# Attention over pooled keys with a gated MLP: first two batches in another order, identity matmuls as steps of their own

## The chip, the core and the metric

The kernel runs on one core of a Trainium2 chip. The core has TensorE (PE, matmuls; its weight loads are listed apart as PEld), VectorE (DVE), ScalarE (ACT), GpSimd (POOL) and SyncE (SP, which here only issues transfers), each with a queue of its own that is worked off in order, and semaphores between them. The metric is the device time of one execution in microseconds, the median of several; lower is better.

## The reference

Inputs are q, k and v (8 batches, 8 heads, 576 tokens, 64 wide) and two weight matrices (512 x 2048 and 2048 x 512), all float32. Keys and values are averaged over groups of 8 tokens, so each head has 72 keys; then attention, then an MLP on the 4608 tokens.

```
k_p = k.reshape(B, H, Sp, pool, D).mean(axis=3)
v_p = v.reshape(B, H, Sp, pool, D).mean(axis=3)
scores = scale * np.matmul(q, k_p.transpose(0, 1, 3, 2))
...
attn = attn / (np.sum(attn, axis=-1, keepdims=True) + 1e-09)
return np.matmul(attn, v_p).astype(np.float32)
...
h = x @ w_in
g = h * (1.0 / (1.0 + np.exp(-1.702 * h)))
return (g @ w_out).astype(np.float32)
```

## The kernel before

**Tiling.** A batch's 512 first tokens are one chunk of the MLP; the 64 left over of each batch make a ninth chunk. Chunks 0 and 1 run through `dense`: for each 128 hidden units f, twelve matmuls `h<-x,w` (three products for each of four quarters of the model width, since both operands are split into a high and a low float32r part), the gelu on ACT, and per 128 tokens three matmuls `o<-w,gh` and `o<-w,gl`. The other chunks take a form with fewer products on pairs of f (`ha`, `hb`, `o<-w,ghall`). Chunk 0 can't begin before batch 0's attention has ended, and the weights for it are decoded on ACT, DVE and POOL as they arrive (`raw`, `e`, `w`).

**Attention of batch 0**, in plain float32 (each matmul is two passes in the trace): `tps` sums the last 64 tokens' keys and values (L1556; DVE makes `tbd` of it); `red_k`, `red_v` sum groups of tokens by matmuls with the identity (L1420; DVE makes `kbd` and `vbd`); `qps` turns the queries (L1699), copied to `qt`; `kps` turns the keys (L1607, L1613), copied by ACT to `k`; `sps` are the scores (L1727); DVE and ACT make the softmax of a piece of the tokens from four `sps` (`nm`, `sc`, `main`, `tail`); `apt` and `tpt` turn the weights (L1871), and `pav` multiplies with the values (L1974, L1977), which become `x`. Names end in batch-free numbers: `sps_0_2` is piece 0, pair of heads 2. Piece 0 has 256 tokens, piece 1 has 320.

**What sets the order.** Every step is a task with an engine and a due time. `Plan.order` lays them out by a planner; then each task's rank is its place in that list plus a number from the table `PLACES`, a table `SWAPPED` moves a step to another engine (a copy from ACT to DVE, a subtraction from POOL to DVE), and the tasks are written out by rank. Each engine's queue follows that order.

**Matmuls of the identity.** `keep_warm` (L2600) multiplies the identity by itself into a bank of PSUM, `warm`, that chunk 0 uses later; nothing reads the product. One such matmul is a task, due first of all. Others are put in as the tasks are written out, ahead of the tasks that `WARMS` names: 16 ahead of `tps`, 2 ahead of the first `qps`, 2 ahead of the first `h`. That makes 21, in the trace 42 passes.

Of the kernel before, what the change touches and what calls it, by code (L numbers as in the profile page):

```python
# [1103 lines left out]
def attention_moe_kernel(ctx: ExitStack, tc: tile.TileContext, q, k, v, w_in, w_out, out):  # L1104
# [1562 lines left out]
    with tc.manual_schedule():  # L2667
        for t in order:
            for _ in range(WARMS.get(t.name, 0)):
                keep_warm()  # L2670
# [31 lines left out]
```

## Time and profile before

| | |
|---|---|
| time, median of 3 runs | 890.97 us (890.58 to 892.03) |
| the profiled execution's own time | 892.42 us |
| its span, first to last instruction | 890.6 us |
| PE busy | 879.3 us (99%) |
| DVE, ACT, POOL busy | 71%, 61%, 35% |

A matmul's record runs on while its result drains, so records of consecutive matmuls overlap: the spacing of their starts is what one costs when they follow each other, and the length of one record is more. A row of the timeline merges consecutive instructions of one kind: its start, the time to the end of the last one, and their count, with the idle time ahead of it in brackets.

### The profile page before, as it was taken

The page shows a single profiled execution, that of the slowest core. Times are in us where ns is not written, and L with a number is a line of the kernel's source. Part 1 is how long each engine was busy: PE and PEld are TensorE (multiplying, and loading weights), DVE is VectorE, ACT ScalarE, POOL GpSimd, SP SyncE. Part 2 cuts the span into 40 slices and gives each one's busy share as a digit, 9 for nine tenths or more (in the row PEclk, how much of TensorE's full clock was granted, in tenths as well). Part 3 has the DMA queues.
Part 4 walks back from the last instruction along what each step waited for, and adds up shares of the span by engine and source line. Part 5 has one row for each costly group of instructions (what it writes and reads, how often), then busy time and mean ns, then how long its engine had stood idle before and what let it go on. Part 6 is the DMA issues. An engine that isn't in the chain of part 4 may idle for free.

```text
span 890.6 us, 15774 instructions
## 1 busy us (share of the span) xinstructions
PE 879.3 (99%) x5432; PEld 785.8 (88%) x5432; DVE 630.1 (71%) x1255; ACT 543.8 (61%) x1245; POOL 314.6 (35%) x309
## 2 busy tenths in 40 slices
PE   7999999999999999999999999999999999999997
PEld 6889988888899998898999998989998989998986
DVE  5877889888888886698878887787677843222332
ACT  4986665356676754667576766686568563344433
POOL 2888565664412233221521161236323460000000
PEclk9999999999999999999999999999999999999999
DMA  9964454657467657678775677667664675556541
GB/s 254 370 223 134 124 151 156 234 200 215 156 202 228 223 181 245 182 226 241 219 218 181 176 233 219 220 203 250 175 205 145 201 235 186 172 190 205 166 142 48
DMA packets 145262, 176.67 MB, mean 198 GB/s; under 512 B 85664, under 2 KB 96928, under 8 KB 145184
## 3 DMA queue, kind: packets, MB, share of 16 engines
q1 hardware_dynamic: 140336, 166.89, 60.5%
q10 hardware_dynamic: 4848, 8.78, 2.8%
q8 instruction: 43, 0.70, 0.3%
q14 instruction: 35, 0.29, 0.1%
HBM read 150.47 MB, written 25.17 MB: 197 GB/s over the span
## 4 chain that ended last, share of the span: by engine, by line
PE 94%; SPq 2%; ACT 1%; DMA 1%; issue 0%; DVE 0%; ACTq 0%
PE ha L2435 18%; PE hb L2435 13%; PE o L2639 12%; PE o L2638 12%; PE o L2637 11%; PE sps L1727 4%; PE h L2230 3%; PE h L2232 3%; PE h L2231 3%; PE o L2274 3%; PE o L2272 3%; PE o L2273 3%; DMA raw<-in_moe_w_out_dram 1%; SPq L1317 1%; PE pav L1966 1%; PE pav L1969 1%
## 5 line engine op out<-in xcount | busy, mean ns | idle before, releaser
L2639 PE MATMUL o<-w,glall 128*128 128x512 f32 x448 | 176.3, 394 | 0.0
L2637 PE MATMUL o<-w,ghall 128*128 128x512 f32 x448 | 176.3, 394 | 0.0
L2638 PE MATMUL o<-w,ghall 128*128 128x512 f32 x448 | 176.0, 393 | 0.0
L2489 POOL TENSOR_TENSOR glall<-shared,ghall 128x256 fp32r<-128x256 f32 x88 | 70.4, 805 | 215.8 <-ACT shared L2482 144.3
L2639 PEld LDWEIGHTS o<-w,glall 128*128 128x128 f32 x448 | 84.2, 188 | 18.5
L2435 PEld LDWEIGHTS ha<-xs,ws 128*128 128x128 f32 x672 | 92.6, 189 | 7.6 <-ACT shared L2450 1.0
L2435 PE MATMUL ha<-xs,ws 128*128 128x256 f32 x672 | 99.2, 283 | 0.0
L2474 ACT ACTIVATE ghall<-shared 128x256 fp32r<-128x256 f32 x150 | 61.5, 415 | 60.9 <-DVE shared L2457 32.5
L2435 PE MATMUL hb<-x,ws 128*128 128x256 f32 x672 | 95.5, 284 | 0.0
L2435 PEld LDWEIGHTS hb<-x,ws 128*128 128x128 f32 x672 | 89.1, 189 | 4.5 <-DVE shared L2457 0.5
L2637 PEld LDWEIGHTS o<-w,ghall 128*128 128x128 f32 x448 | 84.6, 189 | 9.1
L2638 PEld LDWEIGHTS o<-w,ghall 128*128 128x128 f32 x448 | 84.1, 188 | 9.1
L2457 DVE TENSOR_TENSOR shared<-shared,hb 128x256 f32<-128x256 f32 x112 | 46.5, 415 | 55.8 <-PE hb L2435 40.9
L2450 ACT COPY shared<-ha 128x256 f32<-128x256 f32 x94 | 34.8, 370 | 65.0 <-PE ha L2435 63.8
L2489 POOL TENSOR_TENSOR glall<-gall,ghall 128x256 fp32r<-128x256 f32 x45 | 33.4, 746 | 103.4 <-ACT gall L2482 67.9
L2230 PE MATMUL h<-x,w 128*128 128x256 f32 (+1 forms) x192 | 63.0, 328 | 0.7 <-ACT g L2247 0.5
L2482 ACT ACTIVATE shared<-shared 128x256 f32<-128x256 f32 x150 | 61.0, 415 | 3.7 <-ACT osb L2190 0.5
L2232 PE MATMUL h<-x,w 128*128 128x256 f32 (+1 forms) x192 | 61.3, 319 | 0.0
L2231 PE MATMUL h<-x,w 128*128 128x256 f32 (+1 forms) x192 | 61.2, 319 | 0.0
L2260 POOL TENSOR_TENSOR gl<-g,gh 128x512 fp32r<-128x512 f32 x30 | 41.0, 1367 | 50.4 <-ACT gh L2252 35.6
L2489 DVE TENSOR_TENSOR glall<-shared,ghall 128x256 fp32r<-128x256 f32 x62 | 29.5, 477 | 35.8 <-ACT shared L2482 27.3
L2435 PEld LDWEIGHTS ha<-x,shared 128*128 128x128 f32 x336 | 46.7, 189 | 4.8 <-ACT shared L2450 0.8
(193 smaller groups left out, 2039.1 us busy)
## 6 DMA issues: line engine op xcount, KB each, us to landing
ws<-wd SPq DMA_DIRECT2D x168, 512.0 KB
shared<-wd SPq DMA_DIRECT2D x56, 256.0 KB
out_dram<-osb ACTq DMA_DIRECT2D x32, 256.0 KB
wd<-stage SPq DMA_DIRECT2D x16, 512.0 KB
raw<-in_moe_w_in_dram SPq DMA_DIRECT2D x15, 512.0 KB
raw<-in_moe_w_out_dram SPq DMA_DIRECT2D x15, 512.0 KB
kv_False<-in_k_dram SPq DMA_DIRECT2D x28, 256.0 KB
kv_True<-in_v_dram SPq DMA_DIRECT2D x28, 256.0 KB
```

Source lines behind the costliest of these rows:

```text
L2230: nc.tensor.matmul(o, lhsT=w[:, 0, j], rhs=xs[:, 0], start=j == 0, stop=False)
L2231: nc.tensor.matmul(o, lhsT=w[:, 1, j], rhs=xs[:, 0], start=False, stop=False)
L2232: nc.tensor.matmul(o, lhsT=w[:, 0, j], rhs=xs[:, 1], start=False, stop=j == NJ - 1)
L2260: engine.tensor_tensor(out=gl(), in0=g(), in1=gh().bitcast(F32), op=ALU.subtract)
L2435: nc.tensor.matmul(o, lhsT=wv()[:, r, jj], rhs=xo(k, jj), start=start and n == 0, stop=n == len(terms) - 1,  skip_group_check=not start,)
L2457: lambda: nc.vector.tensor_tensor(out=part(i), in0=part(i), in1=hb()[:, half * 256 : half * 256 + 256], op=ALU.add),
L2474: lambda: nc.scalar.activation(out=gh(), in_=src(), func=AF.Gelu_apprx_sigmoid),
L2482: lambda: nc.scalar.activation(out=part(i), in_=src(), func=AF.Gelu_apprx_sigmoid),
L2489: engine.tensor_tensor(out=gl(), in0=part(i), in1=gh().bitcast(F32), op=ALU.subtract)
L2637: nc.tensor.matmul(o(), lhsT=gh()[:, tok], rhs=w()[:, 0], start=start, stop=False)
L2638: nc.tensor.matmul(o(), lhsT=gh()[:, tok], rhs=w()[:, 1], start=False, stop=False)
L2639: nc.tensor.matmul(o(), lhsT=gl()[:, tok], rhs=w()[:, 0], start=False, stop=stop)
```

## The change

The table `WARMS` and its use are gone. `keep_warm` now writes four matmuls instead of one, and 28 such steps are planned, 112 matmuls, where before there were 21. Each step has a place in `PLACES` of its own: steps 0 to 12 have no entry, 13 to 27 have one. The rest of the table is another one for the steps of batches 0 and 1 and of chunk 0, and so is `SWAPPED`.

```diff
-WARMS = {"PE tps0#0": 16, "PE qps0_0#0": 2, "PE h0_0#0": 2}
...
+    "PE tpt0_0#0": -5.6667, "PE tpt1_0#0": 59.8444, "PE tpt1_1#0": 101.0, "PE warm#13": 42.3333,
+    "PE warm#14": 56.3333, "PE warm#15": 96.0, "PE warm#16": 93.2, "PE warm#17": 89.8, "PE warm#18": 101.5,
...
     def keep_warm():
-        nc.tensor.matmul(warm()[:, 0:P], lhsT=ident, rhs=ident, start=True, stop=True)
-
-    pe(WARM, keep_warm, [], [warm], due=-100.0)
+        for _ in range(4):
+            nc.tensor.matmul(warm()[:, 0:P], lhsT=ident, rhs=ident, start=True, stop=True)
+
+    for _ in range(28):
+        pe(4 * WARM, keep_warm, [], [warm], due=-100.0)
...
         for t in order:
-            for _ in range(WARMS.get(t.name, 0)):
-                keep_warm()
             t.emit()
```

On PE the program begins, before, with 17 identity matmuls, and batch 0's keys follow:

```order
L2600 MATMUL warm<-ident 128x128 x17
L1556 MATMUL tps_188<-tl_148,members 128x512
L2600 MATMUL warm<-ident 128x128 x2
L1699 MATMUL qps_0_0_196<-ident,q_0_151 128x128 x2
L1699 MATMUL qps_0_1_199<-ident,q_0_151 128x128 x2
L1607 MATMUL kps_0_202<-ident,kbd_190 128x64x2 x2
L1613 MATMUL kps_0_202<-ident,tbd_192 128x4x8 x2
L1727 MATMUL sps_0_0_215<-k_211,qt_0_0_207 128x144 x2
```

The same place on PE after the change (32 or 33 is added to the lines):

```order
L2633 MATMUL warm<-ident 128x128 x56
L1588 MATMUL tps_220<-tl_195,members 128x512
L2633 MATMUL warm<-ident 128x128 x4
L1731 MATMUL qps_0_0_227<-ident,q_0_214 128x128 x2
L1731 MATMUL qps_0_1_230<-ident,q_0_214 128x128 x2
L1639 MATMUL kps_0_237<-ident,kbd_206 128x64x2 x2
L1645 MATMUL kps_0_237<-ident,tbd_235 128x4x8 x2
L1452 MATMUL red_k_247<-kv_208,ident 128x128 x8
L1759 MATMUL sps_0_0_257<-k_244,qt_0_0_242 128x144 x2
```

Ahead of `tps` now stand 56 identity matmuls instead of 17, and the second half of the keys' sums (`red_k`) has moved up, ahead of the first scores.

On PE between the last scores of batch 0's piece 0 and the turning of its softmax (`apt`), before:

```order
L1727 MATMUL sps_0_2_274<-k_211,qt_0_2_241 128x144 x2
L1727 MATMUL sps_0_3_279<-k_211,qt_0_3_270 128x144 x2
L1420 MATMUL red_v_287<-kv_165,ident 128x128 x8
L1699 MATMUL qps_1_0_309<-ident,q_1_168 128x128 x2
L1699 MATMUL qps_1_0_309<-ident,q_2_170 128x64
L1699 MATMUL qps_1_1_313<-ident,q_1_168 128x128 x2
L1699 MATMUL qps_1_1_313<-ident,q_2_170 128x64
L1420 MATMUL red_v_326<-kv_222,ident 128x128 x8
L1871 MATMUL apt_0_3_360<-ident,main_0_353 128x128 x2
```

The same place on PE after:

```order
L2633 MATMUL warm<-ident 128x128 x12
L1759 MATMUL sps_0_2_310<-k_244,qt_0_2_292 128x144 x2
L1759 MATMUL sps_0_3_323<-k_244,qt_0_3_294 128x144 x2
L2633 MATMUL warm<-ident 128x128 x28
L1731 MATMUL qps_1_1_381<-ident,q_1_351 128x128 x2
L1731 MATMUL qps_1_1_381<-ident,q_2_379 128x64
L1731 MATMUL qps_1_0_387<-ident,q_1_351 128x128 x2
L1731 MATMUL qps_1_0_387<-ident,q_2_379 128x64
L2633 MATMUL warm<-ident 128x128 x4
L1903 MATMUL apt_0_2_403<-ident,main_0_345 128x128 x2
L1903 MATMUL apt_0_3_409<-ident,main_0_345 128x128 x2
L1452 MATMUL red_v_415<-kv_401,ident 128x128 x8
```

Both `red_v` now stand behind `apt`; 12 identity matmuls stand ahead of the scores of head pairs 2 and 3, 28 behind them and 4 ahead of `apt`. Four more stand at each of two later places, ahead of the piece 1 scores of pair 2 and ahead of the last `pav` of piece 0; the two ahead of the first `h` are gone.

All the other float32 matmuls of batch 0 that stood ahead of the first `h` stand ahead of it still. From the last products of chunk 0 on, PE's queue is the same, instruction by instruction, in both.

The SP queue issues the loads; before, it begins:

```order
L2105 DMA raw_131<-in_moe_w_in_dram 128x4x256
L1317 DMA kv_145<-in_k_dram 128x1x512 x2
L1378 DMA tl_148<-in_k_dram 64x8x64
L1378 DMA tl_148<-in_v_dram 64x8x64
L2539 DMA q_0_151<-in_q_dram 128x8x64 x2
L2105 DMA raw_154<-in_moe_w_in_dram 128x4x256
L1317 DMA kv_156<-in_k_dram 128x1x512 x2
```

After:

```order
L2137 DMA raw_131<-in_moe_w_in_dram 128x4x256
L1410 DMA tl_195<-in_k_dram 64x8x64
L1349 DMA kv_201<-in_k_dram 128x1x512 x2
L1349 DMA kv_208<-in_k_dram 128x1x512
L1410 DMA tl_195<-in_v_dram 64x8x64
L2571 DMA q_0_214<-in_q_dram 128x8x64 x2
L1349 DMA kv_208<-in_k_dram 128x1x512
L2137 DMA raw_264<-in_moe_w_in_dram 128x4x256
```

The keys' second half comes ahead of the second block of weights; behind it the queries of piece 1 and the values come after three more blocks of weights.

## Rows read from the trace of the kernel before

**Rows 1.** The page: busy time and share of each engine, and from the 40 slices of the span the busy tenths of PE and the granted clock.

```profile
PE 879.3 (99%) x5432; PEld 785.8 (88%) x5432; DVE 630.1 (71%) x1255; ACT 543.8 (61%) x1245; POOL 314.6 (35%) x309
...
PE   7999999999999999999999999999999999999997
...
PEclk9999999999999999999999999999999999999999
```

**Rows 2.** Busy time by stretch: up to `tps`, up to the first `h`, the rest of chunks 0 and 1 as far as 145 us, and from there to the end. Columns: the stretch and its length, then busy us and count of PE, PEld, DVE, ACT and POOL, the clock, the DMA engines' share, GB/s.

```profile
0.00:8.65 8.65, 6.38 (x34) 6.21 (x35) 2.85 (x12) 1.92 (x2) 0.70 (x6) 1.00 0.74 194
8.65:35.52 26.87, 23.57 (x156) 19.63 (x157) 19.38 (x40) 20.02 (x43) 14.18 (x13) 1.00 1.03 323
35.52:145.00 109.48, 108.74 (x702) 96.94 (x701) 89.69 (x149) 76.90 (x138) 78.61 (x67) 1.00 0.54 167
145.00:890.60 745.60, 740.59 (x4545) 662.97 (x4543) 518.20 (x1056) 444.92 (x1064) 221.09 (x225) 1.00 0.64 199
```

**Rows 3.** What PE waited for: us in total, times, longest. It is the whole list up to 150 us (the same view from 36 us to the end has the `h`, `ha` and `apt` rows only).

```profile
PE warm L2600 <- POOL ident masks.py:199: 1.4, 1, 1.4
PE sps L1727 <- ACT k L1632: 1.2, 2, 0.7
PE red_k L1420 <- DMA kv<-in_k_dram: 1.1, 1, 1.1
PE tps L1556 <- DMA tl<-in_v_dram: 0.9, 1, 0.9
PE h L2230 <- ACT g L2247: 0.5, 1, 0.5
PE qps L1699 <- DVE sps L1784: 0.5, 1, 0.5
PE kps L1607 <- DVE kbd L1452: 0.3, 1, 0.3
PE apt L1871 <- DVE x L2011: 0.2, 1, 0.2
PE h L2230 <- ACT x L2008: 0.2, 1, 0.2
PE kps L1613 <- DVE tbd L1565: 0.2, 1, 0.2
```

**Rows 4.** The first block of identity matmuls in PE's timeline, in two windows: the passes up to 6.1 us and those from 6.5 us on; and all passes of `red_v`, which have the same shape (min, median, max of a record in ns).

```profile
1.36 5.04 PE L2600 MATMUL warm<-ident 128*128 128x128 f32 x22 [1.36 <-POOL ident masks.py:199]
6.35 1.39 PE L2600 MATMUL warm<-ident 128*128 128x128 f32 x11
L1420 PE MATMUL red_v<-kv,ident x32: 275/275/377, 20.0 to 25.4; 128*128 128x128 f32 x32
```

**Rows 5.** PE's timeline from `tps` to the first `h`.

```profile
8.65 1.10 PE L1556 MATMUL tps<-tl,members 128*128 128x512 f32 x2 [0.92 <-DMA tl<-in_v_dram]
9.59 0.61 PE L2600 MATMUL warm<-ident 128*128 128x128 f32 x4
...
13.09 0.66 PE L1727 MATMUL sps<-k,qt 128*128 128x144 f32 x4
14.83 2.02 PE L1420 MATMUL red_k<-kv,ident 128*128 128x128 f32 x16 [1.08 <-DMA kv<-in_k_dram]
...
18.83 1.25 PE L1727 MATMUL sps<-k,qt 128*128 128x144 f32 x8 [0.66 <-ACT k L1632]
19.99 2.02 PE L1420 MATMUL red_v<-kv,ident 128*128 128x128 f32 x16
21.85 0.27 PE L1699 MATMUL qps<-ident,q 128*128 128x128 f32 x1
22.60 1.10 PE L1699 MATMUL qps<-ident,q 128*128 128x128 f32 x5 [0.48 <-DVE sps L1784]
23.63 2.05 PE L1420 MATMUL red_v<-kv,ident 128*128 128x128 f32 x16
25.67 0.63 PE L1871 MATMUL apt<-ident,main 128*128 128x128 f32 x4
...
35.16 0.61 PE L2600 MATMUL warm<-ident 128*128 128x128 f32 x4
35.52 0.36 PE L2230 MATMUL h<-x,w 128*128 128x256 f32 x1
```

**Rows 6.** DMA: the SP queue's load of the second half of the keys in the timeline, bytes by stretch (length, clock, share, GB/s), and from the page's issues the size of each load.

```profile
8.29 1.22 SPq L1317 DMA_DIRECT2D kv<-in_k_dram  x2
2.00:20.00 18.00, 1.00 1.00 283
20.00:40.00 20.00, 1.00 1.04 350
raw<-in_moe_w_in_dram SPq DMA_DIRECT2D x15, 512.0 KB
kv<-in_k_dram SPq DMA_DIRECT2D x4, 256.0 KB
q<-in_q_dram SPq DMA_DIRECT2D x4, 256.0 KB
kv<-in_v_dram SPq DMA_DIRECT2D x4, 256.0 KB
tl<-in_k_dram SPq DMA_DIRECT2D x1, 128.0 KB
```

1666 rows, old and new, of tables (PLACES, SWAPPED) are left out of this document.

## The prediction

> **What bounds the kernel now.** Read first the page's share of the span: PE is busy 99% of it, the next engine 71% [rows 1]. Such an average can hide a stage, so the second view is busy time by stretch [rows 2]. It shows three stages. Up to 8.65 us PE has little but identity matmuls. From there to the first `h` at 35.52 us it is busy 23.57 of 26.87 us. In the rest up to 145 us it is busy 108.74 of 109.48, and from there 740.59 of 745.60, some of the last 5 us being the final stores. So from 35.5 us on the kernel is one unbroken stream of matmuls, and its end moves with the start of that stream almost one for one. Third, the list of PE's waits [rows 3]: between the first block and the first `h` there are seven, 1.2 (two), 1.1, 0.9, 0.5, 0.3 and 0.2, together 4.2 us; after it four, of 1.1 together. That is all that a better order can win. Fourth, PE's timeline around batch 0's attention [rows 5], to see what PE does while others work: behind the last scores (18.83, eight passes) it sums the values (`red_v`, 19.99 and 23.63) and turns queries, and `apt` follows at 25.67 without a wait. The DVE and ACT work of the softmax lies under those steps.
>
> **The change part by part.**
>
> *The identity matmuls.* 112 instead of 21, so 91 more. What one costs comes from the first block [rows 4]. Its first 22 passes take 5.04 us, about 0.22 each: TensorE stood idle before and is at its lower level, 1.2 GHz. In the second window eleven passes take 1.39 us; the last record is 0.275 long (the shortest record of `red_v`, same shape), so ten spacings take 1.115 and one takes 0.1115 us, the upper level, 2.4 GHz. A matmul is two passes, 0.223 us. Both kernels begin the block when the identity is ready, at 1.36 us, so the slow passes are the same in both, and all 91 are paid at the fast price: 91 x 0.223 = 20.3 us. By place: 39 more ahead of `tps` (8.7 us, so `tps` starts at about 16.3 us instead of 8.65), 2 more ahead of the first `qps` (0.4), 12 ahead of the scores (2.7), 28 behind them (6.2), 4 each at three later places (2.7), and 2 fewer ahead of `h` (-0.4).
>
> A rule speaks for a far lower price. The Trainium skill, "TensorE: Matmul & The Clock Gate", section "Back-to-back issue gap", gives columns / 2.4 GHz plus 2.5 ns at the upper level, 56 ns for 128 columns; if that were the whole matmul, 91 would cost an estimated 5.1 us and the sum would come out near zero. The trace disagrees for these float32 operands: two passes of 0.1115 us [rows 4].
>
> Does any of it lie beside other work? On PE nothing lies beside a matmul; it is free only where PE would otherwise wait. So I go through the blocks. *Block of 56:* before, PE waited 0.9 us for `tl` behind 17 matmuls; 39 more take 8.7 us. The block fills that wait and displaces everything behind it. *Block of 12:* it stands where `sps` waited for ACT's `k`; that wait was 0.7 at the longest [rows 3], the block takes 2.7. *Block of 28:* before, the softmax of piece 0 took PE from 19.99 to 25.67 without a stop of more than 0.5 us, since `red_v` filled it [rows 5]. Now both `red_v` stand behind `apt`, and 28 + 4 identity matmuls with the `qps` stand in the gap instead: 32 x 0.223 = 7.1 us plus about 1.1 for the `qps`, 8.2 us against the 5.7 that it took before. They do lie where PE would wait in the new order, but only because the work that filled the gap was moved out of it, and that work (2.02 + 2.05 us) is still to be done ahead of `h`. *Three blocks of 4:* short and among steps that had no wait.
>
> *The waits that go.* With `tps` starting 7.6 us later, the loads are there. At 283 GB/s from 2 us on [rows 6], the second half of the keys ends behind 2.36 MB (a block of weights, both halves of `tl`, the keys, the queries of piece 0: 512 + 2 x 128 + 4 x 256 + 2 x 256 KB), at about 10.3 us, and is needed at about 19; before, it was issued at 8.29 and waited for at 14.83. The queries of piece 1 and the values lie behind 5.1 and 6.2 MB, about 20 and 24 us, and are needed at about 33 and 35. So no wait for a load is left ahead of `h`. `red_k` moved up lies under ACT's `k`, and the block of 12 under the second. I take all seven waits as gone: 4.2 us, and behind each the drain of the record before it, 0.275 - 0.1115 = 0.16, which the waits view counts as busy: 7 x 0.16 = 1.1. Together -5.3 us. Bounds: none goes or as much comes back elsewhere, 0; or these go, the four later ones too (1.1), and the small restarts that no view counts as waits. Of these the eight score passes at 18.83 show one: 1.25 us, where the row of four at 13.09 (0.66) makes it 1.15. Twenty such are 2 us, an estimate. So -8.4 at most.
>
> *The order of the rest.* No matmul but the identity ones was added or dropped, and the float32 work ahead of `h` is the same set. Copies and subtractions change between ACT, DVE and POOL: I cost them at nothing, covered by PE, since ACT and DVE have 6.9 and 7.5 us free in the 26.87 [rows 2] and now get a stretch 15 us longer. If that cover were gone at one place, a wait of the kind in rows 3 would come back, at most 1.2 us. Weights: the loads run on at 350 GB/s [rows 6] while `h` starts 15 us later, so decoding gets ahead of need, not behind.
>
> *Sum.* +20.3 - 5.3 = +15.0 us. The first `h` starts at about 50.5 instead of 35.52. The profiled execution took 892.42 us, 1.45 over the median; 892.42 + 15.0 = 907.4 there, and 890.97 + 15.0 = **906.0** for the median.
>
> **The rivals.**
>
> *More is filled.* The blocks also take the restarts and chunk 0's four waits go, since DVE and ACT are ahead when `h` starts: 20.3 - 8.4 = +11.9, 902.9. For it: rows 3 shows so few waits that a little slack could remove them. Against: restarts come with each change of operand that another engine makes, and those are as many as before.
>
> *The waits stay.* The long block delays the head of a chain (`tps`, `tbd`, `kps`, `k`, `sps`) by 7.6 us and the moved steps meet new waits, so nothing is won back: +20.3, 911.3. For it: five of the seven waits are for DVE and ACT, whose work also starts later. Against: the blocks are longer than each of those waits.
>
> *An identity matmul costs a quarter of its row*, because consecutive ones keep the same stationary operand. The place is the block of 56; at 0.056 us each, 91 cost 5.1, and 5.1 - 5.3 makes 890.8, no change; it decides from a price below 0.06 us. Against: the eleven passes of the first block are in just that situation and cost 0.1115 each.
>
> *Faster: the clock.* If in the timed executions TensorE fell to 1.2 GHz in its waits between 8.65 and 35.5 us, the identity matmuls would buy that back. The place is that stretch; some 18.7 us of other passes lie in it (26.87 less the 5.3, 0.9 of identity matmuls and 2 of restarts), so half the clock there would add up to 18.7; the change then wins 18.7 - 15.0 = 3.7 us, 887.3. It decides from 15 us lost to the clock. Against: passes behind the longest wait keep the upper level (`red_k`, sixteen passes in 2.02 us behind 1.08 of idle [rows 5]), the granted clock is 9 in every slice [rows 1], and the timed runs are shorter than the profiled one, not longer.
> By the Trainium skill, same page, "Part 1: The HAM clock gate", an idle TensorE goes back to 1.2 GHz and activity releases it, which is the reason to place such matmuls. The trace has no wait behind which it fell; none here is longer than 1.1 us.
>
> **How the numbers follow.** Forecast 0.71, more is filled 0.10, the waits stay 0.14, a quarter of the price 0.02, the clock 0.03. The likeliest gives 906.0. The range takes in both bounds of the waits, from 902.5 (902.9, less half a microsecond for the estimate of the restarts) to 911.5; the two cases outside it hold 0.05. A measurement of this kernel tells 0.2% (1.8 us) from no change: faster 0.03, same 0.02, slower 0.95.
>
> **What would show it.** In the profile after: the first block ends at 16.3 us with 22 or 23 slow passes; `tps` starts there with no wait; PE's list of waits ahead of the first `h` is short; the block of 28 takes 6.2 us and `red_v` comes behind `apt`; the first `h` starts near 50.5 us; from there to the end the length is that of before, about 855 us. It would be wrong if identity matmuls were spaced closer than 0.11 us, if the first `h` came at 45 us or earlier, if the stream behind it were shorter by several us, or if new waits of over 2 us stood ahead of it.

## The result, and the profile after

| | before | after |
|---|---|---|
| time, median of 4 runs each | 891.31 us (890.58 to 892.03) | 903.94 us (903.61 to 904.28) |
| the profiled execution's own time | 892.42 us | 903.66 us |
| its span | 890.6 us | 901.9 us |
| start of the first `h` | 35.52 us | 48.56 us |
| from there to the end of the span | 855.0 us | 853.3 us |

The change makes the kernel slower: the ratio of the times is 1.0142, 95% interval 1.0124 to 1.0159, or +12.6 us by the medians and +11.3 us by the two spans.

The page of after, busy time and share of each engine, then PE and the granted clock in 40 slices:

```profile
PE 895.2 (99%) x5614; PEld 805.4 (89%) x5614; DVE 634.3 (70%) x1267; ACT 540.4 (60%) x1236; POOL 307.8 (34%) x304
...
PE   9999999999999999999999999999999999999997
...
PEclk9999999999999999999999999999999999999999
```

Against [rows 1], PE has 182 passes more, which is 91 identity matmuls, and 15.9 us more of busy time. Its share stands at 99% in both, so this number alone doesn't tell the better kernel: work that nothing reads counts as busy. Only the first slice differs, 9 tenths instead of 7.

Busy time by stretch, after: up to 16.3 us, where the prediction had `tps` (it starts at 15.89), up to the first `h`, and up to 145 us (columns as in [rows 2]).

```profile
0.00:16.30 16.30, 14.94 (x113) 14.73 (x114) 5.89 (x15) 2.53 (x3) 3.04 (x8) 1.00 0.88 256
16.30:48.56 32.26, 32.26 (x261) 30.52 (x259) 20.89 (x46) 17.64 (x36) 13.49 (x12) 1.00 0.91 285
48.56:145.00 96.44, 96.06 (x635) 87.06 (x634) 79.06 (x134) 68.85 (x118) 64.47 (x56) 1.00 0.49 143
```

In the second stretch PE is busy 32.26 of 32.26 us; before it was 23.57 of 26.87 [rows 2]. TensorE doesn't wait there at all. PE's list of waits up to 150 us is two rows, against the ten of [rows 3]:

```profile
PE warm L2633 <- POOL ident masks.py:199: 1.4, 1, 1.4
PE pav L2006 <- DVE ah L1981: 0.4, 1, 0.4
```

PE's timeline of after, the rows that answer to [rows 4, 5]:

```profile
1.36 14.70 PE L2633 MATMUL warm<-ident 128*128 128x128 f32 x112 [1.36 <-POOL ident masks.py:199]
15.89 1.02 PE L1588 MATMUL tps<-tl,members 128*128 128x512 f32 x2
...
22.57 2.84 PE L2633 MATMUL warm<-ident 128*128 128x128 f32 x24
25.25 1.15 PE L1759 MATMUL sps<-k,qt 128*128 128x144 f32 x8
26.23 6.41 PE L2633 MATMUL warm<-ident 128*128 128x128 f32 x56
32.48 1.16 PE L1731 MATMUL qps<-ident,q 128*128 128x128 f32 x6
33.57 1.16 PE L2633 MATMUL warm<-ident 128*128 128x128 f32 x8
34.56 0.60 PE L1903 MATMUL apt<-ident,main 128*128 128x128 f32 x4
35.00 1.95 PE L1452 MATMUL red_v<-kv,ident 128*128 128x128 f32 x16
...
48.56 0.38 PE L2262 MATMUL h<-x,w 128*128 128x256 f32 x1
```

The block of 28 begins at 26.23 and the next row at 32.48: 6.25 us for 56 passes, 0.1116 us each, the price of [rows 4]. DVE's timeline shows what goes on beside it, the softmax of piece 0:

```profile
25.94 0.46 DVE L1782 TENSOR_REDUCE nm<-sps 128x4 f32<-128x288 f32 x1 [1.18 <-PE sps L1759]
...
28.46 1.63 DVE L1816 TENSOR_REDUCE sps<-sc 128x8 f32<-128x576 f32 x2
...
31.84 0.75 DVE L1831 TENSOR_TENSOR main<-sc,sps 128x256 f32<-128x256 f32 x2
```

`main` is ready at 32.59, so without the two blocks `apt` would have had to wait for it. With them it starts 1.97 us after that, so they are longer than the wait that they fill. That was the open question: do these matmuls cost their price, or do they fill a wait that the new order has made?

### The profile page after: what moved, and what is told of

Its sections match the earlier page's. It is cut to its first block, busy times and chain, and to the rows that moved or that the text cites. A ratio compares the mean times of both kernels' runs of the same rounds, so it can differ in the third digit from the quotient of the medians.

```text
span 901.9 us, 16133 instructions
## 1 busy us (share of the span) xinstructions
PE 895.2 (99%) x5614; PEld 805.4 (89%) x5614; DVE 634.3 (70%) x1267; ACT 540.4 (60%) x1236; POOL 307.8 (34%) x304
## 4 chain that ended last, share of the span: by engine, by line
PE 97%; ACT 1%; DVE 1%; issue 0%; POOL 0%; ACTq 0%; POOLq 0%
PE ha L2467 18%; PE hb L2467 13%; PE o L2673 11%; PE o L2672 11%; PE o L2671 11%; PE sps L1759 4%; PE warm L2633 3%; PE h L2263 3%; PE h L2264 3%; PE h L2262 3%; PE o L2304 3%; PE o L2305 3%; PE o L2306 3%; PE pav L1998 1%; PE pav L2001 1%; PE pav L2000 1%
## 5 line engine op out<-in xcount | busy, mean ns | idle before, releaser
L2292 POOL TENSOR_TENSOR gl<-g,gh 128x512 fp32r<-128x512 f32 x27 | 37.2, 1377 | 43.9 <-ACT gh L2284 35.8
```

The lines of the kernel that those rows point to most:

```text
L2292: engine.tensor_tensor(out=gl(), in0=g(), in1=gh().bitcast(F32), op=ALU.subtract)
```

## The experiments

**Theory A:** PE is the bound, an identity matmul costs its two passes of 0.1115 us wherever PE would not wait, and nothing where it would; the new order makes a wait of its own, by moving `red_v` behind `apt`. **Against it** stand three: the order of the other steps costs the time and the identity matmuls little; the identity matmuls hold the clock up, so that leaving them out gives back as much as it wins; and waits of a microsecond or two are themselves enough to lower the clock. Experiments on the new order give each of the 28 steps a count; a step with count 0 writes nothing, while its place and all others stay. Only identity matmuls, whose product nothing reads, are left out or added anywhere.

**1. New order, 16 at the start, none later.**

```diff
-    for _ in range(28):
-        pe(4 * WARM, keep_warm, [], [warm], due=-100.0)
+    for i in range(28):
+        pe(4 * WARM, lambda n=4 if i < 4 else 0: keep_warm(n), [], [warm], due=-100.0)
```

> The new order with 16 identity matmuls at the start and none later, 96 fewer. Theory A (PE pays for each identity matmul, and the waits that the blocks covered come back when they go): tps starts when tl lands, near 9.6 us, new waits of 5 to 9 us stand around the softmax of piece 0, where red_v no longer fills the gap; first h between 36 and 40 us, time 889 to 894 us. Rival B (the chain of loads, DVE and ACT in the new order sets the first h, and the blocks lie in its waits): first h stays at 48 to 49 us, 902 to 904 us. Rival C (every matmul is simply paid, no wait comes back): 903.9 - 96 x 0.223 = 882.5 us.

Measured: 895.79 us (5 runs, 893.85 to 896.64), ratio to before 1.0043 [1.0029, 1.0057]; first `h` at 41.69 us. PE's waits:

```profile
PE apt L1903 <- DVE main L1831: 4.0, 1, 4.0
PE tps L1588 <- DMA tl<-in_v_dram: 1.9, 1, 1.9
...
PE qps L1731 <- DVE nm L1782: 1.3, 1, 1.3
PE sps L1759 <- DVE qt L1738: 1.2, 1, 1.2
...
```

And what follows the longest wait, PE's timeline and the stretches between (the clock is the number ahead of the DMA share):

```profile
26.29 1.08 PE L1903 MATMUL apt<-ident,main 128*128 128x128 f32 x4 [4.00 <-DVE main L1831]
27.17 3.62 PE L1452 MATMUL red_v<-kv,ident 128*128 128x128 f32 x16
```

```profile
9.00:10.30 1.30, 0.53 (x2) 0.30 (x2) 1.30 (x1) 0.00 (x0) 0.00 (x0) 1.00 0.76 138
10.30:13.70 3.40, 3.40 (x15) 2.60 (x14) 1.86 (x5) 0.73 (x2) 1.29 (x1) 0.51 1.00 308
13.70:24.00 10.30, 6.07 (x47) 5.23 (x46) 8.05 (x18) 6.56 (x13) 3.88 (x4) 1.00 1.04 299
24.00:30.80 6.80, 4.51 (x22) 4.46 (x23) 2.71 (x8) 2.23 (x6) 4.12 (x4) 0.50 1.03 375
```

The granted clock is 0.51 behind the wait of 1.9 us, and 0.50 from within the wait of 4.0 on: TensorE is at 1.2 GHz, and sixteen `red_v` passes take 3.62 us where after has 1.95. So 96 identity matmuls less, 21.4 us at the row's price, win 8.2 us. A had the wait, but not the clock, and missed its range by 1.8 us. The order by itself isn't the whole cost, since leaving matmuls out wins 8 us; and what the matmuls give back in the clock is less than what they cost.

**2. New order, 56 at the start, none later.** The edit is `i < 14` in the same line.

> The new order with the first block of 56 as it is and the 56 later identity matmuls (12.5 us) left out. Theory A: most of the 12 and the 28 lay in waits which the moved red_v left open, so that only part comes back: first h at 41 to 44 us, 897 to 900 us. Rival B: 902 to 904. Rival C: 903.9 - 12.5 = 891.4.

Measured: 901.21 us (4 runs, 900.53 to 901.83), ratio 1.0107 [1.0092, 1.0122]; first `h` at 46.40 us. PE's waits and timeline:

```profile
PE apt L1903 <- DVE main L1831: 5.1, 1, 5.1
...
PE sps L1759 <- DVE qt L1738: 1.2, 1, 1.2
```

```profile
23.26 1.22 PE L1759 MATMUL sps<-k,qt 128*128 128x144 f32 x8 [1.25 <-DVE qt L1738]
...
30.83 1.09 PE L1903 MATMUL apt<-ident,main 128*128 128x128 f32 x4 [5.09 <-DVE main L1831]
31.71 3.62 PE L1452 MATMUL red_v<-kv,ident 128*128 128x128 f32 x16
```

The 56 later matmuls cost 12.5 us by their price, and leaving them out wins 2.7. The other 9.8: 6.7 us of waits (5.1, 1.2 and two of 0.2), 0.6 of drains ahead of them, and about 2.4 of clock (`red_v` 3.62 for 1.95, `apt` 1.09 for 0.60, some on the two rows behind). A's range was missed by 1.2 us, again for the clock. These blocks do stand in a wait. It is the one that moving `red_v` opened, for the most part (experiment 4 has the shares): before, the same place had `red_v` and no wait [rows 5]. There DVE has `main` ready at 25.53, only 0.14 us ahead of `apt`, so `red_v` and the `qps` just fill the gap:

```profile
24.11 1.42 DVE L1799 TENSOR_TENSOR main<-sc,sps 128x256 f32<-128x256 f32 x4
```

**3. New order, 16 at the start, all later ones kept.** The edit is `i < 4 or i > 13`.

> The new order with the first block cut from 56 to 16 (8.9 us) and the later ones as they are. Theory A: tps starts when tl lands, near 9.6 us instead of 15.9; the later blocks cover what would wait, so 6.3 us of the 8.9 are won, first h near 42.5 us, 896.5 to 899 us. Rival B: 902 to 904. Rival C: 895.0.

Measured: 897.40 us (4 runs, 897.35 to 897.42), ratio 1.0064 [1.0049, 1.0079].

```profile
9.50 1.10 PE L1588 MATMUL tps<-tl,members 128*128 128x512 f32 x2 [1.52 <-DMA tl<-in_v_dram]
```

40 fewer at the start (8.9 us) win 6.5; 1.5 of the rest is the wait for `tl` that is back, and about 1.0 are more slow passes at the start (27, in after 18). As A has it. Here later matmuls follow the wait of 1.5 us without a stop, the granted clock is 1.0 over the run, and `red_k` takes 2.03 us (2.33 in experiment 1).

**4. Old order, 56 at the start.**

```diff
-WARMS = {"PE tps0#0": 16, "PE qps0_0#0": 2, "PE h0_0#0": 2}
+WARMS = {"PE tps0#0": 55, "PE qps0_0#0": 2, "PE h0_0#0": 2}
```

> The order of before with 56 identity matmuls at the start instead of 17, 39 more (8.7 us), the rest as before. Theory A: the waits for loads go (3.0 us with what stands behind them: tl, the keys' second half, the queries), those for DVE and ACT stay: first h at 40.5 to 42 us, 896 to 898 us. Rival B: the long block delays the whole chain and nothing is won back, 900 us. Rival C reads here as all seven waits gone: 891.3 + 8.7 - 5.3 = 894.7 us.

Measured: 897.13 us (4 runs, 896.62 to 897.52), ratio 1.0063 [1.0046, 1.0080]. 39 matmuls (8.7 us) cost 5.8. Of the waits of [rows 3] those for loads (`tps`, `red_k`) are gone. Of the five for DVE and ACT three stay, `sps` twice for ACT's `k` and `kps` for `kbd`; the two of 0.5 and 0.2 us are gone, and one of 0.8 for `main` is new:

```profile
PE sps L1727 <- ACT k L1632: 1.0, 2, 0.5
PE apt L1871 <- DVE main L1799: 0.8, 1, 0.8
...
PE kps L1607 <- DVE kbd L1452: 0.3, 1, 0.3
```

```profile
23.58 1.25 PE L1727 MATMUL sps<-k,qt 128*128 128x144 f32 x8 [0.50 <-ACT k L1632]
...
30.42 0.63 PE L1871 MATMUL apt<-ident,main 128*128 128x128 f32 x4 [0.84 <-DVE main L1799]
```

A later start lets loads catch up, but not a chain that starts with PE's own first result. In the new order these waits are filled by the moved `red_k` and by the later blocks.

These rows also give the shares of the wait in experiment 2, where the same 56 stand at the start. Between the last scores and `apt` PE waits 5.3 us there (5.1 and 0.2) and 0.8 here. Of the 4.5 more, 3.6 are the 32 passes of `red_v` that left the gap (0.1116 each), and 0.7 is the softmax, slower in the new order: from the last scores to `apt`, which waits for `main` in both, it is 7.57 us there and 6.84 here.

**5. Old order, 28 more between the last scores and `apt`,** ahead of the second `red_v`.

```diff
-WARMS = {"PE tps0#0": 16, "PE qps0_0#0": 2, "PE h0_0#0": 2}
+WARMS = {"PE tps0#0": 16, "PE qps0_0#0": 2, "PE red0_v0#0": 28, "PE h0_0#0": 2}
```

> The order of before with 28 identity matmuls more between the last scores of piece 0 and the first red_v, at the place of the block of 28 after. Theory A: there is no wait there while red_v stands in the gap, so they are paid but for the 0.5 us that qps waited: 891.3 + 6.2 - 0.6 = 896.9 us (896.3 to 897.6). Rival B (the gap is a wait of PE in either order): 891 to 892.5 us.

Measured: 896.50 us (4 runs, 895.54 to 897.13), ratio 1.0061 [1.0048, 1.0074], that is +5.5 us for 6.2 us of matmuls. The block stands behind the first `red_v` and the `qps`, not ahead of them as the expectation has it; both places lie in the same gap.

```profile
21.34 6.52 PE L2600 MATMUL warm<-ident 128*128 128x128 f32 x56
27.70 1.95 PE L1420 MATMUL red_v<-kv,ident 128*128 128x128 f32 x16
29.48 0.60 PE L1871 MATMUL apt<-ident,main 128*128 128x128 f32 x4
```

The later blocks are largely free in the new order (experiment 2: 2.7 paid of 12.5 us); 28 of them in the old one are nearly all paid, because `red_v` fills the gap there.

**6. Old order, one identity matmul.**

```diff
-WARMS = {"PE tps0#0": 16, "PE qps0_0#0": 2, "PE h0_0#0": 2}
+WARMS = {}
```

> The order of before with one identity matmul instead of 21. Theory A (the first block's worth is the clock: without it tps and what follows run at 1.2 GHz until TensorE has been busy a while; the four later ones are paid at 0.9 us together): some 4 us of passes at half clock, partly in waits, first h at 36.5 to 39 us, 892.5 to 895.5 us. Rival C (no use in any of them): 890.4 us.

Measured: 892.17 us (10 runs, 890.08 to 892.93), ratio 1.0007 [0.9998, 1.0016]: no difference that the runs tell, though up to 1.4 us more is not excluded (1.1 by the medians).

```profile
7.45 2.05 PE L1556 MATMUL tps<-tl,members 128*128 128x512 f32 x2 [5.29 <-DMA tl<-in_v_dram]
```

`tps` is slow here (2.05 us for 1.10), and so are the passes behind it up to about 11.5 us; but these lie ahead of waits, for ACT's `k` among them, and the first `h` comes at 33.16 us. A, which had 36.5 to 39 for it, was wrong: its time was too high by a little, its first `h` by over 3 us. The 20 identity matmuls that before had beyond the first buy nothing that these runs can tell.

**7. New order, with `red_v` back between the scores and `apt`,** the values' loads ahead again too, and the 28 + 4 left out (80 remain).

```diff
+        pe(4 * WARM, lambda n=0 if 18 <= i <= 25 else 4: keep_warm(n), [], [warm], due=-100.0)
...
+    MOVES = [('DMA raw#2', ['DMA kv0#4', 'DMA kv0#5', 'DMA q0_1#0', 'DMA q0_1#1', 'DMA q0_2#0', 'DMA kv0#6', 'DMA kv0#7']),
+             ('PE sps0_0#3', ['PE red0_v0#0']),
+             ('DVE sps0_0#0', ['DVE vbd0#0', 'PE qps0_1#1', 'ACT qt0_1#1', 'PE qps0_1#0', 'ACT qt0_1#0', 'PE red0_v1#0']),
+             ('DVE main0_0#2', ['DVE vbd0#1'])]
...
```

The list is broken into lines here; the lines left out put the named steps behind the step that each pair begins with.

> The new order, but both red_v (and the loads and DVE steps that belong to them) are put back between the last scores of piece 0 and apt, and the 28 + 4 identity matmuls that stood there are left out; 80 are left. Theory A (those 32 only hold the place of red_v): 32 x 0.223 = 7.1 us less than after, no new wait over 1 us, first h at 41 to 42 us, 896 to 898 us, clock at its upper level throughout. Rival B (the softmax chain on DVE and ACT is the limit whatever PE does there): new waits of 4 us ahead of apt, 900 to 903 us.

Measured: 900.38 us (4 runs, 899.23 to 901.66), ratio 1.0106 [1.0092, 1.0119]: 3.6 us won of 7.1.

```profile
26.53 1.95 PE L1452 MATMUL red_v<-kv,ident 128*128 128x128 f32 x16
...
33.48 0.63 PE L1903 MATMUL apt<-ident,main 128*128 128x128 f32 x4 [2.03 <-DVE main L1831]
```

A wait of 2.0 us for `main` is left, since DVE's softmax is later in this order than in the old one: from the last scores (25.55) to `apt` it is 7.93 us, in experiment 4 6.84. The profiled execution has the clock up throughout, behind this wait too. Two executions with a granted clock of 0.999 and 1.0 took 899.2 and 899.4 us, two with 0.997 took 901.4 and 901.7. The clock did fall in the latter; that this wait, the only one over 0.4 us behind the first block, is where it fell is not shown. A missed its time, its first `h` (44.22) and its "no new wait over 1 us". The time lies in rival B's range, but the wait is half of the one that B names.

**8. The same, 20 at the start and none later.** The edit is `4 if i < 5 else 0`.

> As the kernel with red_v back, with only 20 identity matmuls, all in the first block. Theory A: waits of about 1 us for tl, of 1.2 us for DVE's qt, of up to 1 us ahead of apt, and no clock loss behind them; first h at 34.5 to 36.5 us, and the rest, as in the other runs of the new order, about 1.7 us shorter than before: 888 to 890.5 us, up to 0.3% faster than before. Rival D (waits of that length cost the clock, as they did in the new order with 16): a stretch at half clock, 892 to 895 us.

Measured: 893.53 us (12 runs, 890.47 to 894.34), ratio 1.0022 [1.0013, 1.0032]. PE's waits up to 150 us in the profiled execution (0.2 of the 2.0 lies behind the first `h`):

```profile
PE apt L1903 <- DVE main L1831: 2.0, 2, 1.8
PE tps L1588 <- DVE red_k L1459: 1.6, 1, 1.6
...
PE sps L1759 <- DVE qt L1738: 1.2, 1, 1.2
PE red_v L1452 <- DVE sps L1826: 1.2, 1, 1.2
```

Three of the twelve executions have a clock of 1.0 and took 890.47, 890.73 and 891.62 us; nine have 0.995 to 0.998 and took 893.05 to 894.34. The median lies in the range of the rival that lets short waits cost the clock, and A's range was too low. But the profiled execution is one of the three, with the clock up behind all four of these waits; where it fell in the other nine no trace shows.

**9 and 10. The same, with `main` and `tail` moved ahead of the second `vbd` on DVE,** 24 at the start, and either 4 ahead of the scores of pair 2 and 4 ahead of the second `red_v` (9), or none (10).

```diff
-             ('DVE main0_0#2', ['DVE vbd0#1'])]
+             ('DVE main0_0#2', ['DVE main0_0#1', 'DVE main0_0#0', 'DVE tail0_0#0', 'DVE vbd0#1']),
+             ('ACT qt0_1#0', ['PE warm#18'])]
```

The counts are `4 if i < 6 or i in (15, 18) else 0` in 9 and `4 if i < 6 else 0` in 10.

> As the kernel with red_v back and 20 at the start, with DVE's main and tail ahead of the second vbd, 24 identity matmuls at the start, 4 ahead of the scores of pair 2 and 4 ahead of the second red_v, each in a wait of over 1 us. Theory A: the wait ahead of apt (1.8 us) all but goes, the first h comes at 34 to 35.5 us, 1 to 2 us earlier than in the kernel that it is made from, and the eight later identity matmuls cost nothing: 888.5 to 890.5 us, 0.1% to 0.3% faster than before. Rival: the loads of the values set apt and nothing moves: 890.5 to 893.5.

> The same without the eight identity matmuls in the two waits. Theory A: the waits are there in either case, so the time is that of the kernel with them, within 0.7 us. Rival D (waits of 1.2 us cost the clock in some executions): runs 2 to 4 us longer in part, median 1 to 3 us over the kernel with them.

Measured: 891.79 us (11 runs, 890.30 to 894.43), ratio 1.0011 [1.0002, 1.0020], for 9, and 892.04 us (12 runs, 890.03 to 897.22), ratio 1.0020 [1.0007, 1.0033], for 10. Neither beats before. In 9 the wait ahead of `apt` is gone, as A said, but one of 1.3 us ahead of the next `sps` has come, the first `h` is at 35.72 us, 0.8 earlier than in experiment 8, and the time lies above A's range. In 10 A was right: it is within 0.7 us of 9, so the eight identity matmuls in the two waits neither cost nor win what the runs can tell. In 10's trace the clock is down behind a wait of 1.4 us (PE's timeline and the stretch):

```profile
22.35 2.90 PE L1452 MATMUL red_v<-kv,ident 128*128 128x128 f32 x16 [1.36 <-DVE sps L1825]
25.04 1.06 PE L1903 MATMUL apt<-ident,main 128*128 128x128 f32 x4
```

```profile
23.40:26.40 3.00, 3.00 (x16) 2.90 (x16) 1.91 (x6) 1.85 (x4) 0.32 (x2) 0.50 0.96 354
```

**Where the 12.6 us lie.** In steps, by the medians: after to experiment 3, the matmuls at the start, 6.5; from there to experiment 1, the later ones, 1.6; from there to before, the order of batch 0, 4.5. By way of experiment 2 the first two are 5.4 and 2.7. The last step holds the clock that fell in experiment 1 (the slow `red_v` alone is 1.7 us longer). With `red_v` back and 20 at the start, experiment 8 is 2.5 us over the before of its own runs (891.02); with `main` moved as well and 24, experiment 10 is 1.2 over its own (890.87). So 2.0 of the 4.5 go when `red_v` and the steps that belong to it go back, and 3.3 with DVE's order changed too; what `red_v` alone is worth in it no run separates.

## Why the prediction was right, and where its sum was off

- **PE is the bound and its end moves with the first `h`:** right. The first `h` is 13.0 us later and the span 11.3 us longer.
- **An identity matmul costs 0.223 us:** right, in the first block and in the later ones (0.1116 us a pass in the block of 28).
- **The blocks.** 56 ahead of `tps`: forecast at 16.3, found at 15.89 without a wait, the forecast's 22 slow passes being 18 (the clock rose earlier: the 96 passes from 4.93 us on take 11.12 us, 0.114 each). In the old order 39 more cost 5.8 of 8.7 us. The block of 28: taken as paid since `red_v` was moved out of its gap. Experiments 2, 4 and 5 show it that way: the later blocks are largely free where they stand, in a wait that is there mostly because of the move.
- **The waits that go, "-5.3 us together":** this is the step that was mis-sized. By the profiles 20.3 - 13.0 = 7.3 us came back ahead of the first `h` and another 1.7 behind it; 9.0 in all, 0.6 beyond the bound of -8.4. By the medians it is 20.3 - 12.6 = 7.7, and that is the fairer figure, since the profiled execution of before was 1.1 us over the median of its four runs: experiment 5, whose PE queue is the same up to 21 us, has no wait ahead of `red_k` and starts `tps` at 7.98. In the profiles all seven waits went, as counted (4.2, and 1.1 for the drains); 0.4 is the earlier clock; the last 1.5 ahead of `h` are the small restarts, which stood in the bound and not in the value (this part is by subtraction, no row shows it alone).
- **"From there to the end the length is that of before":** 1.7 us shorter. The four waits behind the first `h` (1.1) became two, of 0.4 and 0.2; with the drains that makes 0.8, and where the other 0.9 lies no row here shows. It belongs to the new order, not to the matmuls: behind the first `h` experiments 7, 8 and 10 take 853.3, 853.3 and 853.2 us, experiments 4 and 6 in the old order 854.9 and 855.1. Experiment 9 loses it again (855.3) with a wait of 1.3 us for DVE's `al`.
- **The rivals.** "More is filled", 902.9, with a chance of 0.10, came nearest, in mechanism and in time: 903.94 is 1.0 us from it and 2.1 from the forecast of 906.0, which had 0.71. The direction, the price and the place were worked out; that the time lies in the range is owed to its taking in both bounds of the waits. "The waits stay" fell: no wait is left ahead of `h`. The quarter of the price fell by the spacing. The clock fell as a rival, since with one identity matmul before is no slower (experiment 6). But its mechanism is real, and the argument "no wait behind which it fell" held only for the waits of that trace: behind 1.4 us and more it did fall in the traces of experiments 1, 2 and 10.

## What to carry to other kernels

On the engine that bounds the kernel, filler work is free only inside a wait that is there already, and in no run here did it win time that the runs can tell; look for the wait at that very place in the trace and don't count on fillers at places where real work lies. If fillers seem to be free, ask what was moved to make room for them: here they stood in a wait that the same change had opened. With the real work back in it and most of the fillers left out the time came to between 891.8 and 893.5 us; with the fillers alone left out, to 895.8 at best. Order real, independent matmuls into such a gap first, and judge fillers by the time of the first instruction of the unbroken stream, not by the share of busy time.

## What the runs showed of the hardware that was not expected

TensorE fell to 1.2 GHz behind waits shorter than the prediction thought to matter: the granted clock is 0.51 from 10.3 us on in experiment 1, behind a wait of 1.9 us, and 0.50 in experiment 10, around `red_v`, which waited 1.36 us and had been preceded by little work. It was up again at 13.7 and 26.7 us. The length of the wait doesn't decide it. In before, 1.1 us of idle ahead of `red_k` left the clock up [rows 5], in experiment 3 so did 1.5 us with dense passes behind it, and in the trace of experiment 7 so did 2.0 us. It varies between executions of one kernel, too: in experiment 8 the clock was 1.0 in three and 0.995 to 0.998 in nine, and the median of the nine is 3.1 us longer (893.8 against 890.7). The clock isn't the whole of the spread: the profiled execution of experiment 10, with its fall, is the second fastest of its twelve, and experiment 6 has 890.1 to 892.9 us with a clock of 1.0 in all ten.

By the Trainium skill, "TensorE: Matmul & The Clock Gate", "Why this matters for your kernels", only longer gaps than these are to be avoided. The runs disagree: behind gaps of 1.4 and 1.9 us the clock fell.

The slow passes at the start of a kernel are not a fixed number either: 22 in before [rows 4], 18 in after. Experiments 2, 4 and 7 begin with the same 56 identity matmuls as after and have 16, 14 and 21. By the Trainium skill, "TensorE: Matmul & The Clock Gate", "Part 1: The HAM clock gate", this count differs between runs of one kernel. No kernel here has two traces, but those that begin alike agree with it. The slow start has to be read from the spacing of the passes: the clock column reads 1.00 there too, as in the first stretch of [rows 2]. In experiment 6, where it falls on `tps` and what follows, it costs nothing that the runs can tell.
